# Five output buffers, an earlier split of x, and six more TensorE transposes in a windowed attention and two feed-forward layers

## The chip, the cores and the metric

The kernel runs on one core of a Trainium2 chip. The metric is the device time of one execution in microseconds (us). Three timed runs of the kernel before lie between 959.54 and 962.82 us, with a median of 962.39.

## The reference, cut to what matters

All data are fp32 (the weights of the two layers arrive as fp64). Attention looks back over 64 positions; its output, 2304 tokens of 512 values, goes through a feed-forward layer with 2048 inner columns and then through a gated one with 1536.

```python
scores = q @ k.T / sqrt(64); masked to 0 <= i - j < 64      # 4 batches, 8 heads, 576 positions
x = softmax(scores) @ v                                     # -> 2304 x 512
h = x @ w_in; x = (h * sigmoid(1.702 * h)) @ w_out          # layer A
xn = x / sqrt(mean(x * x) + 1e-6) * rms_g                   # layer B
out = (silu(xn @ w_gate) * (xn @ w_val)) @ w_out2
```

## The kernel before, in words

Every fp32 operand of a large product is kept as a high and a low part, and each product is three matmuls (high by high, high by low, low by high).

**Who sets the order.** All work is entered as operations with a cost per engine, a priority and the buffers they use. `Planner.emit` plays the program through with these costs and writes each engine's instructions in the order in which they start there. On the chip each engine then goes through its own list in that order and stops at the first instruction that must wait. SP's list holds the loads and stores; POOL's list holds, beside arithmetic, the loads of weights that are used a second time (`again`).

**Layer A** runs over six token blocks `j` (512, 256 and four of 384 tokens), with 16 steps each. Attention for the groups of 64 tokens of block `j` is laid among the matmuls of block `j - 1`. Groups are numbered 0 to 35: block 2 is groups 12 to 17, block 3 is 18 to 23. For one group TensorE computes the scores (L426), VectorE masks and reduces them (L451, L456), ScalarE takes the exponential (L461), POOL divides (L470), the probabilities are turned, and TensorE multiplies by v (L485). For groups below `NPE` = 18 the turning is four TensorE transposes into a PSUM bank (L475) and one copy out of it. From group 18 on it is a VectorE transpose in 32 by 32 squares (L518) and some ten small copies on ScalarE and POOL that put the squares in place (L310 and L312 with the tile `pts`). Along with this, the fp64 weights of layer B come in as `raw`, are narrowed on ScalarE and VectorE (L338, L342, L346, L352) and stored to DRAM as `wp` (gate and value weights, one for each unit) and `wr` (output weights). At the end of each block `a_finish` stores x and, by L704, L695 and L698, one word per token that holds its norm (`ms`, `ss`, `rs`).

**Layer B** runs over three blocks of 768 tokens, with 12 units each; even units are gates, odd ones values. The gate and value products use a scheme with seven products in place of eight (p = 0 to 6, L877 to L879, tile `bank`, two PSUM banks). Each unit thus needs seven combinations of x, prepared in `words` (`b_prep`) and split by `b_splits` into high and low parts (L310 and L808, 768 columns). The first copy after product 0 is `th<-bank` on ScalarE (L310); it frees the bank that product 2 needs. After two units, `b_down` adds their share to six accumulators of 128 tokens (L978 to L980; four tiles `y` in PSUM, two `abank`). After a block's last unit `b_finish` copies each accumulator, halved, to an SBUF tile of kind `y` (L995 on ScalarE or L997 on VectorE; there are two such tiles) and stores it (L1000).

In the first block of layer B the weights of unit n come from DRAM as fp32 (`fw<-wp`, 1 MB, L847; two buffers `fw`), are split into their frames (L310, L819; `slab` for even n, `late` for odd n), and the split form is stored as `wc` (L833) for the later blocks, which read it back by POOL's list (L837).

Of the kernel before, what the change touches and what calls it, by code (L numbers as in the profile page):

```python
# [9 lines left out]
F32 = mybir.dt.float32  # L10
# [13 lines left out]
class Buf:  # L24
    __slots__ = ("kind", "tile", "left", "users")

    def __init__(self, kind):
        self.kind, self.tile, self.left, self.users = kind, None, 0, 0
# [178 lines left out]
def window_attention_two_moe_kernel(ctx: ExitStack, tc: tile.TileContext, ins, out):  # L207
# [20 lines left out]
    NPE = gbase[3]  # L228
# [37 lines left out]
        "xa": (None, 2, [P, NK, P], F32),  # L266
        "y": (ring, 2, [P, 512], F32),
# [26 lines left out]
    def make(b):  # L294
# [8 lines left out]
        b.tile = p.tile(shape, dt, tag=b.kind, name=b.kind, bufs=n)  # L303
# [442 lines left out]
    def b_prep(j, t, prio, after):  # L746
        bufs = []
        for half in range(2):
# [3 lines left out]
            xb, rb = Buf("xa"), Buf("sq")  # L752
# [4 lines left out]
            def load_r(e, rb=rb, ja=ja, src=src):  # L757
                nc.sync.dma_start(out=make(rb)[:, 0, 0:P], in_=rs_d[ja][:, src].to_broadcast([P, P]))
# [3 lines left out]
            pl.op({"D": 0.45}, load_r, prio - 1, r=[("rs", ja)], new=[rb], after=after)  # L762
# [36 lines left out]
    def b_splits(prio):  # L799
        for p in range(7):  # L800
            hf, lf = XF + 2 * p, XF + 2 * p + 1
            st = [("st", p, t) for t in range(HT // P)]

            def hi_(e, p=p, hf=hf):
                copy("A", flat(hf), words(STAGE + p)[:, 0:2 * HT])

            def lo_(e, p=p, hf=hf, lf=lf):
                eng[e].tensor_tensor(out=flat(lf), in0=words(STAGE + p)[:, 0:2 * HT], in1=flat(hf).bitcast(F32),  # L808
                                     op=ALU.subtract)

            pl.op({"A": act(2 * HT)}, hi_, prio + p / 7, r=st, w=ftok(hf))
            pl.op(both(2 * HT), lo_, prio + p / 7, r=st + ftok(hf), w=ftok(lf), port="GV")
# [23 lines left out]
    def again(d, f, n, tok, key, prio):  # L836
        pl.op({"G": 1.2}, lambda e: nc.gpsimd.dma_start(out=frame(f)[:, :, 0:n], in_=d), prio, r=[key], w=tok,  # L837
              late=3.0)

    def b_weights(n, prio, after=()):  # L840
# [6 lines left out]
        pl.op({"D": dma(P * 8192)}, lambda e: nc.sync.dma_start(out=make(fb), in_=w32p_d[n]), prio - 0.4, new=[fb],  # L847
# [7 lines left out]

    def b_out_weights(q, prio, after=()):
        for i in range(2):
            c, f = (2 * q + i) % NB, WO + i
            if 2 * q >= NB:
# [4 lines left out]
                  prio + i - 0.4, new=[fb], r=[("w32d", "o", c), "at closed"], after=after)  # L864
# [239 lines left out]
    def ex_open(e):  # L1104
        actx.close()
        p = ctx.enter_context(tc.tile_pool(name="ex", bufs=1, side="right", reuse_waits="tile"))
        for kind in ("sb", "fw"):
            KINDS[kind] = (p, *KINDS[kind][1:])
# [124 lines left out]
```

## Time and profile before

| | |
|---|---|
| median of the timed runs | 962.39 us |
| profiled execution, its own time | 956.81 us |
| span of the trace in that execution | 955.0 us |
| busy: TensorE, VectorE, ScalarE, POOL | 912.2, 652.7, 432.7, 275.1 us |
| DMA, mean over the span | 204 GB/s |

The trace begins 1.8 us short of the execution's own time. TensorE (PE in the rows) is the engine that is nearly always busy; its idle time and the stretches with a lower granted clock (PEclk, 1.00 is 2.4 GHz and 0.50 is 1.2 GHz) are what a change can win. Layer A ends and layer B begins at about 500 us; layer B's second block begins near 660 us and its third near 810 us.

### The profile page before, as it was taken

The page shows a single profiled execution, that of the slowest core. Times are in us where ns is not written, and L with a number is a line of the kernel's source. Part 1 is how long each engine was busy: PE and PEld are TensorE (multiplying, and loading weights), DVE is VectorE, ACT ScalarE, POOL GpSimd, SP SyncE. Part 2 cuts the span into 40 slices and gives each one's busy share as a digit, 9 for nine tenths or more (in the row PEclk, how much of TensorE's full clock was granted, in tenths as well). Part 3 has the DMA queues.
Part 4 walks back from the last instruction along what each step waited for, and adds up shares of the span by engine and source line. Part 5 has one row for each costly group of instructions (what it writes and reads, how often), then busy time and mean ns, then how long its engine had stood idle before and what let it go on. Part 6 is the DMA issues. An engine that isn't in the chain of part 4 may idle for free.

```text
span 955.0 us, 15401 instructions
## 1 busy us (share of the span) xinstructions
PE 912.2 (96%) x5436; PEld 843.4 (88%) x5436; DVE 652.7 (68%) x1240; ACT 432.7 (45%) x1075; POOL 275.1 (29%) x389
## 2 busy tenths in 40 slices
PE   8999999997999999999999989998999999899997
PEld 7777789997999999899999978887999998799996
DVE  5999974474877688674477878775676567565553
ACT  6667564465566566555346333453222233222222
POOL 4111021133444345331013433372222233122210
PEclk9999999999999999999999999999899999999999
DMA  8756533357565676761759898788777676776752
GB/s 284 241 172 208 168 109 67 108 136 221 199 221 164 220 255 213 192 215 53 125 180 312 223 358 304 302 300 261 213 226 235 200 199 181 225 212 207 204 145 95
DMA packets 86536, 194.63 MB, mean 204 GB/s; under 512 B 12726, under 2 KB 36027, under 8 KB 84924
## 3 DMA queue, kind: packets, MB, share of 16 engines
q1 hardware_dynamic: 66108, 137.02, 44.5%
q0 software_dynamic: 20352, 56.63, 20.3%
q8 instruction: 43, 0.70, 0.3%
q14 instruction: 33, 0.27, 0.1%
HBM read 140.13 MB, written 53.50 MB: 203 GB/s over the span
## 4 chain that ended last, share of the span: by engine, by line
PE 41%; DMA 6%; DVE 3%; issue 1%; ACT 1%; POOL 1%; SPq 0%; ACTq 0%; POOLq 0%; DVEq 0%
PE bank L877 7%; PE bank L879 7%; PE bank L878 7%; DMA out_dram<-y 3%; PE y L978 3%; PE y L980 3%; PE y L979 3%; PE y L626 1%; DMA wc<-late 1%; PE y L627 1%; PE y L628 1%; PE bank L552 1%; PE bank L554 1%; PE bank L553 1%; PE abank L978 1%
## 5 line engine op out<-in xcount | busy, mean ns | idle before, releaser
L552 PE MATMUL bank<-xh,slab 128*128 128x384 f32 (+2 forms) x288 | 99.2, 345 | 0.5 <-DVE th L609 0.5
L554 PE MATMUL bank<-xh,slab 128*128 128x384 f32 (+2 forms) x288 | 97.2, 338 | 1.9 <-DVE slab L379 1.9
L553 PE MATMUL bank<-xl,slab 128*128 128x384 f32 (+2 forms) x288 | 97.6, 339 | 0.5 <-DVE xl L492 0.5
L626 PE MATMUL y<-gh,slab 128*128 128x384 f32 (+2 forms) x288 | 98.0, 340 | 0.0
L628 PE MATMUL y<-gh,slab 128*128 128x384 f32 (+2 forms) x288 | 96.8, 336 | 0.5 <-DVE slab L379 0.5
L627 PE MATMUL y<-gl,slab 128*128 128x384 f32 (+2 forms) x288 | 96.6, 335 | 0.0
L310 ACT ACTIVATE xh<-sb 128x384 fp32r<-128x384 f32 x72 | 36.1, 522 | 113.9 <-DVE sb L930 113.9
L878 PE MATMUL bank<-slab,late 128*128 128x384 f32 x252 | 86.8, 345 | 0.0
L902 DVE TENSOR_TENSOR gh<-gl,bank 128x384 f32<-128x384 f32 x108 | 59.3, 550 | 37.4 <-PE bank L879 37.0
L878 PE MATMUL bank<-slab,slab 128*128 128x384 f32 x252 | 84.5, 335 | 0.0
L915 ACT ACTIVATE sb<-gh 128x384 f32<-128x384 f32 x72 | 37.6, 524 | 103.3 <-DVE gh L902 103.2
L609 DVE SCALAR_TENSOR_TENSOR th<-th,bank 128x384 f32<-128x384 f32 (+2 forms) x96 | 52.6, 547 | 43.6 <-ACT th L605 43.3
L605 ACT ACTIVATE th<-bank 128x384 f32<-128x384 f32 (+2 forms) x96 | 46.4, 484 | 60.3 <-PE bank L554 53.1
L470 POOL TENSOR_TENSOR e<-e,rc 128x512 f32<-128x512 f32 x34 | 37.0, 1088 | 122.4 <-DVE rc L467 106.3
L877 PE MATMUL bank<-slab,late 128*128 128x384 f32 x180 | 63.2, 351 | 8.6 <-ACT th L310 7.8
L877 PE MATMUL bank<-slab,slab 128*128 128x384 f32 x180 | 61.6, 342 | 6.9 <-DVE gl L902 5.3
L310 ACT ACTIVATE gh<-th 128x384 fp32r<-128x384 f32 (+2 forms) x96 | 50.2, 524 | 39.0 <-DVE th L609 35.5
L879 PE MATMUL bank<-slab,late 128*128 128x384 f32 x180 | 62.5, 347 | 0.0
L338 ACT ACTIVATE raw<-raw 128x512 f32<-128x512 f32 x68 | 46.1, 680 | 33.1 <-DMA raw<-in_w_gate_dram 10.7
L879 PE MATMUL bank<-slab,slab 128*128 128x384 f32 x180 | 60.6, 337 | 0.0
L902 DVE TENSOR_TENSOR gl<-gl,bank 128x384 f32<-128x384 f32 x72 | 39.8, 552 | 28.2 <-PE bank L879 25.4
L554 PEld LDWEIGHTS bank<-xh,slab 128*128 128x128 f32 x288 | 54.3, 189 | 4.7 <-DVE slab L379 2.7
(169 smaller groups left out, 2567.3 us busy)
## 6 DMA issues: line engine op xcount, KB each, us to landing
slab<-wc POOLq DMA_DIRECT2D x36, 512.0 KB, 4.6
late<-wc POOLq DMA_DIRECT2D x36, 512.0 KB, 4.2
wp<-raw SPq DMA_DIRECT2D x24, 512.0 KB, 5.4
fw<-wp SPq DMA_DIRECT2D x12, 1024.0 KB, 7.6
late<-wo POOLq DMA_DIRECT2D x24, 512.0 KB, 5.3
q<-in_q_dram SPq DMA_DIRECT2D x36, 256.0 KB, 4.5
wc<-slab SPq DMA_DIRECT2D x18, 512.0 KB, 5.2
wc<-late SPq DMA_DIRECT2D x18, 512.0 KB, 4.3
```

The source lines that it names most:

```text
L310: nc.scalar.activation(out=out, in_=in_, func=AF.Copy)
L552: nc.tensor.matmul(h, w[:, 0, kk], xh_ring[:, kk, cols], start=(kk == 0), stop=False)
L553: nc.tensor.matmul(h, w[:, 0, kk], xl_ring[:, kk, cols], start=False, stop=False)
L554: nc.tensor.matmul(h, w[:, 1, kk], xh_ring[:, kk, cols], start=False, stop=(kk == NK - 1))
L609: nc.vector.scalar_tensor_tensor(out=th, in0=th, scalar=1.0, in1=hb.tile[:, 0:n], op0=ALU.add, op1=ALU.mult)
L626: nc.tensor.matmul(y, s[:, 0, cols], hb.tile[:, 0:n], start=first, stop=False)
L627: nc.tensor.matmul(y, s[:, 0, cols], lb.tile[:, 0:n], start=False, stop=False)
L628: nc.tensor.matmul(y, s[:, 1, cols], hb.tile[:, 0:n], start=False, stop=last)
L877: nc.tensor.matmul(h, w[:, 0, kk], xh[:, kk], start=kk == 0, stop=False)
L878: nc.tensor.matmul(h, w[:, 0, kk], xl[:, kk], start=False, stop=False)
L879: nc.tensor.matmul(h, w[:, 1, kk], xh[:, kk], start=False, stop=kk == 1)
L902: nc.vector.tensor_tensor(out=(make(to) if kind else s.tile)[:, 0:HT].bitcast(F32), in0=s.tile[:, 0:HT].bitcast(F32), in1=b.tile[:, 0:HT], ...
```

## The change

Six things are edited.

1. `NPE` goes from group 18 to group 24, so the probabilities of token block 3 are turned on TensorE.
2. Results go through five SBUF tiles in turn (one `o`, two `y`, two `sq`) and are copied by ScalarE alone.
3. The norms that layer B loads have tiles of their own (`rs`), where they used `sq` before.
4. Combinations 0 and 1 of x for the second and third block of layer B are split one unit earlier. For the second block they go into the two `fw` buffers, which are free by then; the third block finds its own frames free.
5. The last two output weights go, by POOL's list, into an `fw` buffer.
6. The planner is told other costs and priorities: `fw<-wp` ranks a unit earlier, `y<-wr` 0.8 units earlier, and a POOL load costs 0.6 in place of 1.2.

```diff
-    NPE = gbase[3]
+    NPE = gbase[4]
...
+        "rs": (None, 2, [P, 1, P], F32),
+        "o": (None, 1, [P, 512], F32),
         "y": (ring, 2, [P, 512], F32),
...
-            xb, rb = Buf("xa"), Buf("sq")
+            xb, rb = Buf("xa"), Buf("rs")
...
-            pl.op({"D": 0.45}, load_r, prio - 1, r=[("rs", ja)], new=[rb], after=after)
+            pl.op({"D": 0.45}, load_r, prio - 1, r=[("rs", ja), "at closed"], new=[rb], after=after)
...
+    xbuf = {}
+
+    def xplace(j, p, lane):
+        if (j, p) in xbuf:
+            f = xbuf[j, p].tile.rearrange("p h c l -> p (h c l)")
+            return f[:, lane * 2 * HT:(lane + 1) * 2 * HT]
+        return flat(XF + 2 * p + lane)
+
+    def xtok(j, p, lane):
+        if (j, p) in xbuf:
+            return [xbuf[j, p], (xbuf[j, p], "low")][lane:lane + 1]
+        return ftok(XF + 2 * p + lane)
+
+    def b_split(j, p, prio):
+        st = [("st", p, t) for t in range(HT // P)]
+        if j == 1 and p < 2:
+            xbuf[j, p] = Buf("fw", F32R)
+        new = [xbuf[j, p]] if (j, p) in xbuf else []
+
+        def hi_(e):
+            if new:
+                make(new[0])
+            copy("A", xplace(j, p, 0), words(STAGE + p)[:, 0:2 * HT])
+
+        def lo_(e):
+            eng[e].tensor_tensor(out=xplace(j, p, 1), in0=words(STAGE + p)[:, 0:2 * HT],
+                                 in1=xplace(j, p, 0).bitcast(F32), op=ALU.subtract)
+
+        pl.op({"A": act(2 * HT)}, hi_, prio, r=st, w=() if new else xtok(j, p, 0), new=new)
+        pl.op(both(2 * HT), lo_, prio, r=st + xtok(j, p, 0), w=xtok(j, p, 1), hold=new, port="GV")
...
-        pl.op({"G": 1.2}, lambda e: nc.gpsimd.dma_start(out=frame(f)[:, :, 0:n], in_=d), prio, r=[key], w=tok,
+        pl.op({"G": 0.6}, lambda e: nc.gpsimd.dma_start(out=frame(f)[:, :, 0:n], in_=d), prio, r=[key], w=tok,
...
-        pl.op({"D": dma(P * 8192)}, lambda e: nc.sync.dma_start(out=make(fb), in_=w32p_d[n]), prio - 0.4, new=[fb],
+        pl.op({"D": dma(P * 8192)}, lambda e: nc.sync.dma_start(out=make(fb), in_=w32p_d[n]), prio - 1.4, new=[fb], late=3.0,
...
+        if q == NBB * NU // 2 - 1:
+            wb = wobuf[q] = Buf("fw", F32R)
+            pl.op({"G": 0.01}, lambda e: make(wb), prio - 2, new=[wb])
+            for f in range(2):
+                c = (2 * q + f) % NB
+                pl.op({"G": 0.6}, lambda e, f=f, c=c: nc.gpsimd.dma_start(out=wplace(q, f), in_=wo_d[c]), prio - 2,
+                      r=[("wo", c), wb], w=[(wb, f)], late=3.0)
+            return
...
-                  prio + i - 0.4, new=[fb], r=[("w32d", "o", c), "at closed"], after=after)
+                  prio + i - 1.2, new=[fb], r=[("w32d", "o", c), "at closed"], after=after, late=2.0)
...
+    outs = []
+
     def b_finish(j, t, a, prio):
-        ob = Buf("y")
+        ob = Buf(("o", "y", "sq", "y", "sq")[len(outs) % 5])
+        outs.append(ob)
         r0 = j * BT + t * P
+        def flat_out():
+            return ob.tile.rearrange("p a c -> p (a c)") if ob.kind == "sq" else ob.tile
+
         def out_(e):
-            if e == "A":
-                nc.scalar.activation(out=make(ob), in_=a.tile, func=AF.Copy, scale=0.5)
-            else:
-                nc.vector.tensor_scalar(out=make(ob), in0=a.tile, scalar1=0.5, scalar2=None, op0=ALU.mult)
-
-        pl.op({"A": act(512, False), "V": dve(512)}, out_, prio, r=[a], new=[ob])
-        pl.op({"D": dma(P * 2048)}, lambda e: nc.sync.dma_start(out=out[r0:r0 + P], in_=ob.tile), prio, r=[ob])
+            make(ob)
+            nc.scalar.activation(out=flat_out(), in_=a.tile, func=AF.Copy, scale=0.5)
+
+        pl.op({"A": act(512, False)}, out_, prio, r=[a], new=[ob])
+        pl.op({"D": dma(P * 2048)}, lambda e: nc.sync.dma_start(out=out[r0:r0 + P], in_=flat_out()), prio, r=[ob])
...
+        if j + 1 < NBB and u == NU - 2:
+            for p in range(2):
+                b_split(j + 1, p, SA + n + 0.6 + p / 7)
         if j + 1 < NBB and u == NU - 1:
-            b_splits(SA + n + 0.7)
+            for p in range(2, 7):
+                b_split(j + 1, p, SA + n + 0.7 + p / 7)
```

The order of ScalarE's list at the end of layer B's first block, before. `y<-y` and `y<-abank` are the copies of results (L995), `th<-bank` is the copy that frees a bank after product 0, `sb<-gh` and `xh<-sb` belong to the unit's own arithmetic.

```order
L310 ACTIVATE th<-bank 128x384
L310 ACTIVATE xh<-sb 128x384 x2
L995 ACTIVATE y<-y_6062 128x512
L915 ACTIVATE sb<-gh 128x384 x2
L995 ACTIVATE y<-abank 128x512
L995 ACTIVATE y<-y_6134 128x512
L915 ACTIVATE sb<-gh 128x384 x2
L995 ACTIVATE y<-y_6154 128x512
L310 ACTIVATE th<-bank 128x384
```

The same place in the changed kernel; L1036 are the copies of results.

```order
L312 ACTIVATE th<-bank 128x384
L1036 ACTIVATE o<-y_6008 128x512
L1036 ACTIVATE y<-abank 128x512
L1036 ACTIVATE sq<-abank 128x512
L312 ACTIVATE xh<-sb 128x384
L1036 ACTIVATE y<-y_6087 128x512
L312 ACTIVATE xh<-sb 128x384
L1036 ACTIVATE sq<-y_6106 128x512
L312 ACTIVATE xh<-sb 128x384
L1036 ACTIVATE o<-y_6126 128x512
L312 ACTIVATE th<-bank 128x384
```

All six copies now stand in ScalarE's list (four did before), still ahead of the next `th<-bank`, and only the sixth takes a tile that an earlier one of the six has used.

SP's list in layer B's first block, before, from a store of unit 3's split weights to the load of unit 5's weights (`wp5`); `wc4` are the stores of unit 4's split weights.

```order
L833 DMA wc3_3_170<-late3_1306 128x1024
L698 DMA rs5_130<-ss_6128 128x3x1
L863 DMA y_6196<-wr3_146 128x512
L833 DMA wc4_0_171<-slab5_87 128x1024
L833 DMA wo2_205<-late5_1308 128x1024
L833 DMA wc4_1_172<-slab10_92 256x1x256
L833 DMA wc4_2_173<-slab7_89 128x1024
L833 DMA wc4_3_174<-slab12_94 128x1024
L847 DMA fw_6275<-wp5_136 128x2048
```

The same place in the changed kernel.

```order
L700 DMA rs5_130<-ss_6068 128x3x1
L851 DMA wc3_3_170<-late3_1306 128x1024
L865 DMA fw_6160<-wp5_136 128x2048
L851 DMA wo2_205<-late5_1308 128x1024
L898 DMA y_6206<-wr4_147 128x512
L851 DMA wc4_0_171<-slab5_87 128x1024
L851 DMA wc4_1_172<-slab10_92 256x1x256
L851 DMA wc4_2_173<-slab7_89 128x1024
L851 DMA wc4_3_174<-slab12_94 128x1024
```

The load of unit 5's weights moves ahead of the four stores of unit 4's.

VectorE's list ahead of group 20's mask, before: from the end of group 19's arithmetic (`rc`) to L451. L342 is the first VectorE step on a fresh `raw` weight.

```order
L467 RECIPROCAL rc_2611<-rc_2611 128x4
L609 SCALAR_TENSOR_TENSOR th_2609<-th_2609,bank_2564 128x384
L567 TENSOR_TENSOR gl_2632<-th_2609,gh_2630 128x384
L518 STREAM_TRANSPOSE t1_2634<-e_2579 128x512
L609 SCALAR_TENSOR_TENSOR th_2650<-th_2650,bank_2617 128x384
L567 TENSOR_TENSOR gl_2684<-th_2650,gh_2682 128x384
L342 TENSOR_SCALAR raw_2636<-raw_2636 128x512
L346 SCALAR_TENSOR_TENSOR raw_2636<-raw_2636 128x512
L609 SCALAR_TENSOR_TENSOR th_2697<-th_2697,bank_2665 128x384
L352 SCALAR_TENSOR_TENSOR raw_2636<-raw_2636 128x512
L492 TENSOR_TENSOR xl_75<-abank_2688,xh_74 128x4x64
L451 SCALAR_TENSOR_TENSOR e_2728<-abank_2703,m_rest_77 128x512
```

The same place in the changed kernel, where L344 is that first step and L453 the mask.

```order
L469 RECIPROCAL rc_2596<-rc_2596 128x4
L354 SCALAR_TENSOR_TENSOR raw_2455<-raw_2455 128x512
L611 SCALAR_TENSOR_TENSOR th_2599<-th_2599,bank_2558 128x384
L569 TENSOR_TENSOR gl_2620<-th_2599,gh_2605 128x384
L611 SCALAR_TENSOR_TENSOR th_2629<-th_2629,bank_2607 128x384
L569 TENSOR_TENSOR gl_2649<-th_2629,gh_2647 128x384
L344 TENSOR_SCALAR raw_2622<-raw_2622 128x512
L348 SCALAR_TENSOR_TENSOR raw_2622<-raw_2622 128x512
L494 TENSOR_TENSOR xl_75<-abank_2651,xh_74 128x4x64
L453 SCALAR_TENSOR_TENSOR e_2687<-abank_2664,m_rest_77 128x512
```

The VectorE transpose is gone, and the steps on the fresh weight still stand ahead of the mask. In TensorE's list 60 matmuls of 384 columns stand between group 20's scores and its product with v before; in the changed kernel there are 48, the four transposes, and 12 more.

## Rows read from the trace of the kernel before

**Rows 1.** TensorE's waits, whole span: us in total, times, longest us.

```profile
PE bank L877 <- ACT th L310: 8.8, 3, 4.2
...
PE bank L877 <- DVE gl L902: 5.3, 5, 3.1
```

**Rows 2.** Busy us by engine in stretches, granted clock, DMA share, GB/s.

```profile
150.00:200.00 50.00, 47.73 (x436) 45.85 (x436) 22.65 (x54) 24.45 (x84) 8.82 (x9) 1.00 0.38 109
235.60:241.40 5.80, 5.02 (x30) 4.74 (x31) 4.51 (x7) 3.47 (x8) 2.11 (x4) 0.51 0.85 282
500.00:650.00 150.00, 144.66 (x749) 132.20 (x748) 116.08 (x197) 68.96 (x131) 63.09 (x57) 1.00 0.88 301
668.50:674.70 6.20, 6.16 (x19) 6.17 (x20) 1.95 (x5) 0.00 (x0) 0.53 (x1) 0.50 0.80 247
677.00:795.00 118.00, 117.58 (x611) 109.06 (x612) 79.19 (x162) 31.45 (x59) 31.70 (x53) 1.00 0.75 214
814.70:818.10 3.40, 3.40 (x13) 3.40 (x12) 0.74 (x2) 0.00 (x0) 0.56 (x1) 0.50 0.30 84
948.40:955.00 6.60, 0.01 (x1) 0.00 (x0) 0.00 (x0) 1.75 (x3) 0.00 (x0) 0.71 0.41 159
```

**Rows 3.** Chain that ended last, 650 to 670 us: start, us, what.

```profile
656.28 4.37 DMA out_dram<-y
...
661.38 6.02 DMA out_dram<-y
...
667.50 0.60 ACT y L995
...
668.54 0.69 PE bank L877
```

**Rows 4.** ScalarE's timeline, 804 to 828 us: start, us, operation, [idle before, releaser].

```profile
812.67 0.60 ACT L995 ACTIVATE y<-abank 128x512 f32<-128x512 f32 x1 [4.12 <-DMA out_dram<-y]
...
825.35 0.60 ACT L995 ACTIVATE y<-y 128x512 f32<-128x512 f32 x1 [2.70 <-DMA out_dram<-y]
```

**Rows 5.** Chain that ended last, 940 to 955 us.

```profile
948.98 2.00 DMA out_dram<-y
...
951.08 0.60 ACT y L995
```

**Rows 6.** Chain that ended last, 540 to 558 us.

```profile
544.45 9.99 DMA fw<-wp
...
554.54 0.67 ACT late L310
...
557.05 0.44 PE bank L877
```

**Rows 7.** SP's timeline, 195 to 245 us.

```profile
209.29 0.39 SPq L698 DMA_DIRECT2D rs<-ss  x1
...
210.28 0.86 SPq L1136 DMA_DIRECT2D wp<-raw  x2
221.59 0.33 SPq L334 DMA_DIRECT2D raw<-in_w_val_dram  x1
```

**Rows 8.** All engines' timeline, 222 to 242 us.

```profile
225.19 0.43 DVE L342 TENSOR_SCALAR raw<-raw 128x512 int32<-128x512 int32 x1 [6.04 <-DMA raw<-in_w_val_dram]
...
232.00 1.08 POOL L470 TENSOR_TENSOR e<-e,rc 128x512 f32<-128x512 f32 x1 [2.43 <-DVE rc L467]
...
235.68 0.45 PE L485 MATMUL abank<-pts,v 128*64 128x64 f32 x2 [4.10 <-POOL pts L312]
```

**Rows 9.** TensorE's waits from 185 to 280 us.

```profile
PE abank L485 <- POOL pts L312: 4.8, 2, 4.1
```

**Rows 10.** TensorE's timeline, 142 to 168 us.

```profile
143.21 0.60 PE L475 MATMUL abank<-ident,e 128*128 128x128 f32 x4
143.56 0.36 PE L626 MATMUL y<-gh,slab 128*128 128x256 f32 x1
...
163.79 0.66 PE L475 MATMUL abank<-ident,e 128*128 128x128 f32 x4 [0.71 <-POOL e L470]
```

More of the change, by code (lines that the diff above doesn't have):

```diff
@@ L24, with __init__ @@
 class Buf:
-    __slots__ = ("kind", "tile", "left", "users")
-    def __init__(self, kind):
-        self.kind, self.tile, self.left, self.users = kind, None, 0, 0
+    __slots__ = ("kind", "tile", "left", "users", "dt")
+    def __init__(self, kind, dt=None):
+        self.kind, self.tile, self.left, self.users, self.dt = kind, None, 0, 0, dt
 class Op:
@@ L302, in make @@
         p, n, shape, dt = KINDS[b.kind]
-        b.tile = p.tile(shape, dt, tag=b.kind, name=b.kind, bufs=n)
+        b.tile = p.tile(shape, b.dt or dt, tag=b.kind, name=b.kind, bufs=n)
         return b.tile
@@ L854, in b_weights, with wplace, wtok @@
             keep(wc_d[n][f], base + f, WIDTH[f], ftok(base + f), ("wc", n, f), prio + 0.3)
-    def b_out_weights(q, prio, after=()):
+    wobuf = {}
+    def wplace(q, f):
+        return wobuf[q].tile[:, f].rearrange("p c l -> p (c l)").rearrange("p (s c) -> p s c", s=2) if q in wobuf else \
+            frame(WO + f)
+    def wtok(q, f):
+        return [wobuf[q], (wobuf[q], f)] if q in wobuf else ftok(WO + f)
+    def b_out_weights(q, prio, after=()):
+        if q == NBB * NU // 2 - 1:
[6 more added lines that the diff above has]
+            return
         for i in range(2):
@@ L874, in fn @@
             w = frame(wf)[:, :, o:o + 256].rearrange("p s (k f) -> p s k f", k=2)
-            xh, xl = block(hf), block(lf)
+            xh, xl = (xplace(j, p, lane).rearrange("p (k c) -> p k c", k=2) for lane in range(2))
             for kk in range(2):
@@ L879, in fn @@
                 nc.tensor.matmul(h, w[:, 1, kk], xh[:, kk], start=False, stop=kk == 1)
-        return pl.op({"T": 6 * mmcost(HT)}, fn, prio, r=ftok(wf) + ftok(hf) + ftok(lf), new=[hb])
+        return pl.op({"T": 6 * mmcost(HT)}, fn, prio, r=ftok(wf) + xtok(j, p, 0) + xtok(j, p, 1), new=[hb],
+                     hold=[xbuf[j, p]] if (j, p) in xbuf else ())
     halfsets = {}
@@ L970, in b_down, with fn @@
             hi, lo = uset(q, f, h)
-            wf = WO + f
             key = ("u", q % 2, f, h)
-            def fn(e, f=f, t=t, tt=tt, hi=hi, lo=lo, wf=wf):
-                s = frame(wf)
+            def fn(e, f=f, t=t, tt=tt, hi=hi, lo=lo):
+                s = wplace(q, f)
                 sl = slice(tt * P, (tt + 1) * P)
@@ L1106, in ex_open @@
         p = ctx.enter_context(tc.tile_pool(name="ex", bufs=1, side="right", reuse_waits="tile"))
-        for kind in ("sb", "fw"):
+        for kind in ("sb", "fw", "rs", "o"):
             KINDS[kind] = (p, *KINDS[kind][1:])
@@ L1166, in window_attention_two_moe_kernel @@
         a_down(s)
-    b_splits(SA - 3)
+    for p in range(7):
+        b_split(0, p, SA - 3 + p / 7)
     b_weights(1, SA - 0.5, [ups[SA - 6]])
```

17 lines of the change are left out of this document (3 added, 14 removed).

## Prediction

> **What bounds the kernel now.** I read TensorE's waits first, since that engine is nearly always busy. Two entries bear on layer B [rows 1]: three waits of together 8.8 us that end when ScalarE's `th<-bank` copy has freed a bank, the longest 4.2, and five of together 5.3 us that end with a VectorE sum, the longest 3.1. Next come the stretches with their granted clock [rows 2]. Between 677 and 795 us, inside the second block, TensorE is busy 117.58 of 118 us: away from the changes of block nothing is to be won. From 500 to 650 us, the first block, it is busy 144.66 of 150 us while the DMA engines are 88% busy at 301 GB/s. In three short stretches the clock stands at half (1.2 of 2.4 GHz): 235.6 to 241.4, 668.5 to 674.7 and 814.7 to 818.1 us. Each follows a wait, and while it lasts TensorE does half its work, so they cost about 2.8, 3.1 and 1.7 us beside the waits. The last row is the tail: 6.6 us after the last matmul.
>
> Then the chain shows what the waits hang on. At the end of the first block [rows 3] a store of a result lands after 4.37 us, the next copy takes the tile it has freed, that copy's store takes 6.02 us, and only when a third copy has had its tile (667.50) does `th<-bank` follow on the same engine and TensorE go on at 668.54. At the end of the second block ScalarE twice stands before a result copy until a store has landed, 4.12 and 2.70 us [rows 4]. So a wait for an SBUF tile becomes a wait for a PSUM bank, because ScalarE works in order.
>
> **The change part by part; the sum is made against the profiled execution, 956.8 us.**
>
> *Five tiles for results.* Only a block's sixth copy takes a tile used by one of the same block, and that copy comes a whole unit's results after the first, behind a store of some 4 to 6 us [rows 3]. So the three `th` waits go, 8.8 us [rows 1], and with them the two slow stretches after them, 3.1 + 1.7 us [rows 2]. That is 13.6 us. It is not more, since what stands between is matmuls. If the sixth copy still waits at both places I would keep half of it, 6.8. That ScalarE now copies all eighteen costs nothing: a copy is 0.60 us [rows 3], eighteen are 11 us in the whole span, and ScalarE is busy only 31.45 of 118 us in a steady stage [rows 2].
>
> *The tail.* Now the last copy (951.08) waits for a store of 2.00 us, ends at 951.7, its own store at 953.7, and the span at 955.0 [rows 5, 2]. With a free tile the last copy starts with the last matmul's end, 948.4: 0.6 + 2.0 + the same 1.3 make 3.9 us in place of 6.6. Gain 2.7; nothing excludes 1 less if the six copies queue.
>
> *Weights a unit earlier.* In the first block, unit 5's load is issued at 544.45 and lands 9.99 us later, the split follows at 554.54, and TensorE goes on at 557.05 [rows 6]. That is the 3.1 us wait. In the changed order this load stands before unit 4's four stores, so it can go about when they begin rather than after them; a few microseconds are enough. I take the 3.1 and leave the other four waits of that entry (2.2 us together). The DMA engines carry the same bytes, so no gain beyond 5.3 is open here; the loss is a rival below.
>
> *Six groups' transposes on TensorE.* Four transposes start at 143.21, and the next matmul at 143.56 [rows 10]; this matmul is also some 0.09 us slower to give way, so a group costs 0.44 us, six cost 2.6 us. What they replace lay on VectorE, ScalarE and POOL, which wait for others more than they are waited for; its removal is worth only what TensorE waited for the small copies: 4.8 us in this stage [rows 9], and the slow stretch after it, 2.8 us [rows 2]. Here I do not follow the label. Both waits are group 20's, and the row of VectorE shows where it began: idle for 6.04 us until a `raw` weight landed, at 225.19, ahead of this group's mask in its list; the division thus started only at 232.00 [rows 8]. The weight's load was issued at 221.59, when `wp` stores issued at 210.28 had given its buffer back, and these followed the one-word-per-token store `rs` of 209.29 [rows 7]. All of that order is kept, and the fresh weight is still ahead of the mask. So TensorE will now stop at the transposes instead of at `pts`. The division ends at 233.1, the transposes take 0.35 us and the copy is covered by 12 matmuls, so TensorE is free at 233.5. Before, the product with v could begin at 235.68 [rows 8], waited 0.7 again (4.8 in two waits, the first 4.1 [rows 9]) and was free at about 236.8: 3.3 us later. But the 12 matmuls that now follow the transposes were done before the wait until now, 2.3 us at 118 us for 611 matmuls in the steady stretch, 0.19 each [rows 2]. Net gain 1.0 us, with the slow clock kept. The other five groups get less room (36 or 48 matmuls between scores and transposes where 54 to 74 stood before v). Block 2's groups have that form already, and one of them waited 0.71 us for the division [rows 10]. I take 1.0 us for all five. Together +2.6 - 1.0 + 1.0 = +2.6. Bounds: if the weight lands in time, 2.6 - 4.8 - 2.8 = -5.0; if each of the five waits the 0.71, 2.6 - 1.0 + 3.6 = +5.2.
>
> On transposes the Trainium skill ("TensorE: Matmul & The Clock Gate", Part 4: PE-mode transpose) says that they do not count as work for the clock. From 150 to 200 us, with block 2's transposes among the matmuls, the granted clock is 1.00 [rows 2], so this trace does not agree; what the rule would cost is priced among the rivals.
>
> *The rest.* Two combinations split a unit ahead, the norms' own tiles, the last output weights in an `fw` buffer: the same number of instructions, at another place. The cover is a steady unit's matmuls, with 0.4 us of waits in 118 [rows 2]; I count 0. Without cover each would be a wait of the kind of the 1 to 3 us ones above.
>
> Sum: -13.6 - 2.7 - 3.1 + 2.6 = -16.8, so 940.0 for a profiled execution. The median of the runs, 962.4, stands 5.6 above the profiled one; I carry that over: **945.6 us**, 1.8% less.
>
> **The rivals.**
>
> *Group 20's wait goes as well.* If the small store lands sooner by chance of timing, the transposes are worth 5.0 where I booked a loss of 2.6: 938. For it: nothing but timing; against it: the kept order.
>
> *Stores still hold ScalarE.* If they are slower, or issued late because SP's list has loads before them, the sixth copy or the second waits, and half of the 13.6 stays: 952. Stores of 4.37 and 6.02 us beside weight loads speak for it, five tiles against it.
>
> *DMA becomes the bound of the first block (slower than before).* 88% busy leaves little. A load of 1 MB pulled ahead puts the stores of split weights back by 1 MB at 301 GB/s, 3.3 us; two units later the same frame is split again and must wait for its store. If units 4 to 11 each paid it, 8 x 3.3 = 26 us against 17 won: 972. It decides from about the sixth unit that pays. Against it: two units are 23 us (a unit has 42 matmuls of products and 18 of accumulation, 0.19 us each), far more than 3.3.
>
> *The clock.* If six groups' transposes each brought a half-clock stretch like that at 235.6 us, 2.8 us each, 17 us would be lost, in place of the one such stretch kept in the sum: 960. The Trainium skill's rule above would do this; the stretch from 150 us speaks against it.
>
> *Nothing much happens.* A new wait of ScalarE or POOL at the block changes takes most of it back: within 0.5%.
>
> **How the numbers follow.** The forecast (941 to 950) has 0.50, group 20 gone too 0.17, stores still waiting 0.12, a gain of some 6 to 9 us from several small losses 0.09, nothing much 0.06, the clock 0.02, DMA bound 0.04. 0.5%, 4.8 us, is about what a measurement of this kernel can tell from no change. Faster: 0.50 + 0.17 + 0.12 + 0.09 = 0.88. Same: 0.06 + 0.02 = 0.08. Slower: 0.04. The range reaches from a little under the second case to a little over the third, 934 to 956.
>
> **What would show it.** In the changed trace: no wait of TensorE that ends with `th<-bank` near 660 and 810 us, the clock at 1.00 there, and no result copy of ScalarE that waits for `out_dram`; a tail of about 4 us; no wait of 3 us near 554 us; a wait for the division of 3 to 5 us at group 20 before L477's transposes, with a half-clock stretch behind it; TensorE's matmuls longer by 24 transposes. I am wrong if result copies still end with a store, if layer A grows by more than 6 us, or if the first block of layer B shows waits for `wc` stores.

## The result, and the profile after

The changed kernel took 945.4 us (median of four, 944.01 to 945.68) beside 960.96 for the kernel before: ratio 0.9845, interval 0.9801 to 0.9888. Measured again in a later comparison (e5 below) it took 950.26 us, ratio 0.9886, 0.9864 to 0.9909. So it is faster by 1.1 to 1.6%, and the forecast of 945.6 was met by the first measurement; the second lies just above the 941 to 950 that I gave the forecast. Its parts were not met, as the rest shows: layer B gained more than I gave it, layer A lost more.

TensorE's waits over the whole span (total, times, longest) answer to [rows 1]:

```profile
PE abank L477 <- POOL e L472: 5.8, 2, 4.9
...
PE bank L912 <- ACT th L312: 1.9, 2, 1.7
PE bank L912 <- DVE gh L938: 1.8, 2, 0.9
...
PE bank L912 <- DVE gl L938: 0.4, 1, 0.4
```

The waits for `th<-bank` went from 8.8 us to 1.9, those for a sum to `gl` from 5.3 to 0.4. In their place the first row is group 20's wait for the division, 4.9 us, where it was forecast. I had forecast no `th` wait near 660 us; one of 1.7 us is left there (655.4 to 657.1). The stretches answer to [rows 2] (busy us by engine, granted clock, DMA share, GB/s):

```profile
150.00:189.00 39.00, 39.00 (x375) 38.19 (x375) 17.00 (x40) 18.98 (x68) 6.73 (x7) 1.00 0.34 94
193.40:196.80 3.40, 3.40 (x15) 3.40 (x15) 1.80 (x3) 0.54 (x3) 0.00 (x0) 0.50 0.63 157
234.40:237.80 3.40, 3.18 (x12) 3.18 (x13) 2.76 (x5) 1.01 (x2) 0.17 (x1) 0.50 0.78 286
377.70:381.20 3.50, 3.50 (x15) 3.50 (x16) 2.28 (x5) 0.52 (x1) 0.40 (x1) 0.51 0.84 278
408.50:411.90 3.40, 3.40 (x14) 3.40 (x15) 3.37 (x7) 1.44 (x4) 2.33 (x3) 0.50 0.36 95
500.00:650.00 150.00, 147.48 (x772) 136.28 (x771) 120.67 (x209) 72.93 (x139) 57.52 (x54) 1.00 0.87 295
650.00:670.00 20.00, 18.15 (x93) 16.18 (x92) 15.21 (x22) 6.48 (x12) 7.98 (x10) 1.00 0.73 215
677.00:795.00 118.00, 118.00 (x615) 109.86 (x614) 77.47 (x154) 32.00 (x60) 35.05 (x57) 1.00 0.78 234
805.00:825.00 20.00, 20.00 (x105) 18.55 (x105) 11.40 (x23) 7.47 (x14) 4.04 (x8) 1.00 0.93 288
939.30:943.80 4.50, 0.04 (x1) 0.00 (x0) 0.00 (x0) 0.60 (x1) 0.00 (x0) 1.00 0.50 188
```

At both block changes (650 to 670 and 805 to 825 us) the clock is now 1.00 and at the second nothing waits. The tail is 4.5 us in place of 6.6. But layer A, which had one stretch at half clock after its first 30 us, has four. Where layer A ends is read from the second `ones` matmul of each block, the last step of TensorE on a block's norms. Layer B's first products already stand before the last of these; in every run of the table below 2072 to 2074 matmuls follow it, so the mark has the same place in all of them. Before, and after (number, then duration in ns, first and last start):

```profile
L684 PE MATMUL abank<-gl,ones x6: 279/334/394, 143.0 to 525.0; 128*128 128x384 f32 x4, 128*128 128x512 f32 x1, 128*128 128x256 f32 x1
```

```profile
L686 PE MATMUL abank<-gl,ones x6: 282/336/443, 144.3 to 535.0; 128*128 128x384 f32 x4, 128*128 128x512 f32 x1, 128*128 128x256 f32 x1
```

With the durations of these last ones layer A ended 10.1 us later, layer B (from there to the last matmul) took 404.0 in place of 423.1 us, and the tail 2.1 less: together, up to rounding, the 11.2 us between the two spans. The experiments' traces, read in the same way (us; the last column is the ratio of the timed executions to the kernel before of the same comparison):

| run | end of layer A | layer B | tail | ratio, 95% |
|---|---|---|---|---|
| before | 525.3 | 423.1 | 6.6 | 1 |
| changed | 535.4 | 404.0 | 4.5 | 0.9845 (0.9801 to 0.9888) |
| e2 transposes alone | 536.1 | 425.8 | 6.6 | 1.0064 (1.0040 to 1.0089) |
| e3 five tiles alone | 523.7 | 413.0 | 4.0 | 0.9904 (0.9877 to 0.9932) |
| e4 loads earlier alone | 531.4 | 418.1 | 6.6 | 0.9924 (0.9899 to 0.9950) |
| e5 changed again | 538.3 | 406.1 | 4.4 | 0.9886 (0.9864 to 0.9909) |
| e6 changed, no transposes | 533.3 | 406.4 | 4.0 | 0.9815 (0.9795 to 0.9834) |
| e7 changed, rs from POOL | 530.4 | 404.3 | 4.0 | 0.9794 (0.9776 to 0.9812) |
| e8 both of these | 532.8 | 404.0 | 4.0 | 0.9771 (0.9747 to 0.9795) |
| e11 e6, no early splits | 530.0 | 419.8 | 4.0 | 0.9936 (0.9911 to 0.9960) |
| e12 e6, rs in rows and later | 512.5 | 403.9 | 4.0 | 0.9586 (0.9561 to 0.9611) |

Two things are to be seen. Layer B repeats to within 3 us between kernels that share its code (404.0, 406.1, 406.4, 404.3, 404.0, 403.9; before and e2, 423.1 and 425.8), so its column can be read from one trace with that uncertainty. Layer A does not: up to the end of its fifth block the kernel before and e4 have the same instructions in the same order on every engine, yet that block ended at 447.9 us in the one trace and at 454.1 in the other. What an edit does to layer A is taken from the ratios alone.

### The profile page after: what moved, and what is told of

Read it like the earlier page. It is cut to its first block, busy times and chain, and to the rows that moved or that the text cites. A ratio compares the mean times of both kernels' runs of the same rounds, so it can differ in the third digit from the quotient of the medians.

```text
span 943.8 us, 15339 instructions
## 1 busy us (share of the span) xinstructions
PE 912.6 (97%) x5460; PEld 845.6 (90%) x5460; DVE 647.1 (69%) x1241; ACT 426.9 (45%) x1039; POOL 253.3 (27%) x350
## 4 chain that ended last, share of the span: by engine, by line
PE 63%; DVE 15%; DMA 12%; ACT 5%; issue 2%; POOL 1%; SPq 0%; ACTq 0%; DVEq 0%; POOLq 0%
PE bank L912 8%; PE bank L913 8%; PE bank L914 8%; DMA wp<-raw 4%; PE bank L556 3%; PE bank L554 3%; PE bank L555 3%; PE y L1013 3%; PE y L1015 3%; PE y L1014 3%; PE y L628 3%; PE y L630 3%; PE y L629 3%; DVE raw L348 2%; PE abank L428 2%
## 5 line engine op out<-in xcount | busy, mean ns | idle before, releaser
L628 PE MATMUL y<-gh,slab 128*128 128x384 f32 (+2 forms) x288 | 99.6, 346 | 0.8 <-DVE y L653 0.8
L630 PE MATMUL y<-gh,slab 128*128 128x384 f32 (+2 forms) x288 | 97.2, 338 | 0.7 <-DVE slab L381 0.7
L913 PE MATMUL bank<-slab,late 128*128 128x384 f32 x228 | 77.1, 338 | 0.0
L913 PE MATMUL bank<-slab,slab 128*128 128x384 f32 x228 | 76.5, 336 | 0.0
L340 ACT ACTIVATE raw<-raw 128x512 f32<-128x512 f32 x68 | 46.3, 683 | 35.6 <-DMA raw<-in_w_gate_dram 10.9
L463 ACT ACTIVATE e<-e,nm 128x128 f32<-128x128 f32 x112 | 43.6, 392 | 38.6 <-DVE nm L458 37.0
L569 DVE TENSOR_TENSOR gl<-th,gh 128x384 fp32r<-128x384 f32 (+2 forms) x77 | 44.8, 581 | 22.4 <-ACT gh L312 21.9
L556 PEld LDWEIGHTS bank<-xh,slab 128*128 128x128 f32 x288 | 55.0, 191 | 5.4 <-DVE slab L381 3.3
L555 PEld LDWEIGHTS bank<-xl,slab 128*128 128x128 f32 x288 | 55.2, 192 | 2.6 <-DVE xl L494 0.6
L554 PEld LDWEIGHTS bank<-xh,slab 128*128 128x128 f32 x288 | 55.4, 192 | 2.1 <-ACT slab L312 0.2
```

Source lines behind the costliest of these rows:

```text
L554: nc.tensor.matmul(h, w[:, 0, kk], xh_ring[:, kk, cols], start=(kk == 0), stop=False)
L555: nc.tensor.matmul(h, w[:, 0, kk], xl_ring[:, kk, cols], start=False, stop=False)
L556: nc.tensor.matmul(h, w[:, 1, kk], xh_ring[:, kk, cols], start=False, stop=(kk == NK - 1))
L628: nc.tensor.matmul(y, s[:, 0, cols], hb.tile[:, 0:n], start=first, stop=False)
L630: nc.tensor.matmul(y, s[:, 1, cols], hb.tile[:, 0:n], start=False, stop=last)
L913: nc.tensor.matmul(h, w[:, 0, kk], xl[:, kk], start=False, stop=False)
```

## The experiments

### One part at a time

**Without the transposes (e1, and e6 for a trace).**

```diff
-    NPE = gbase[4]
+    NPE = gbase[3]
```

> The changed kernel, but the six groups of the fourth token block have their probabilities transposed on VectorE again. Three theories, against 945.4 us of the changed kernel. (a) The prediction's term: the transposes cost 2.6 us net, so 942.8, and layer A, which in the changed trace ends 8.4 to 9 us later than before, ends some 6 us later still. (b) All that layer A lost comes with the transposes: 936 to 937, no stretch at half clock near 377 and 408 us, layer A's last value product within 1 us of the kernel before. (c) The transposes are worth their 5.0 us and something else delays layer A: 948 to 951. What would settle it beside the time: the end of layer A in its trace.

Ratio 0.9788 (0.9763 to 0.9813), 941.9 us. I take no reading from this run's trace; e6 is the same kernel beside the changed one:

> The changed kernel with the six groups' probabilities transposed on VectorE again, once more, for a trace. Expected: 941 to 943, 4 to 6 us below the changed kernel beside it. If the cost of the transposes lies in their own six groups, the two traces part between 202 and 290 us and run level afterwards; if it lies in later groups (copies of probabilities on ScalarE behind a weight that has not landed, near 318 and 405 us), they part after 300 us.

It took 944.04 us, and the changed kernel beside it 950.26: 6.2 us, 0.0071 in the ratio. **The other way round, the transposes alone in the kernel before (e2):**

> The kernel before with the one edit that the fourth token block's six groups transpose on TensorE. Against some 961 us of the kernel before: (a) by the prediction's term 963.6; (b) if the transposes are what made layer A 8.4 to 9 us longer, 969 to 970, all of it before 525 us; (c) if the wait of group 20 goes with the small copies, 956. Group 20 should wait for the division before its transposes in (a) and (b).

968.64 against 962.86 us, so 5.8 us, near theory (b) and not (a). Three comparisons (5.5 from e1's ratio against the changed kernel's own, then 6.2 and 5.8) agree: the transposes cost about 6 us, not 2.6. The size stood just above my upper bound of 5.2. It lies in layer A: e2's layer B and tail are those of before within what a trace repeats (2.7 us and none). The two traces do not part in one place: between 203 and 456 us TensorE's waits sum to 12.5 us in e5, with the transposes, and to 10.9 in e6.

**Five result tiles alone (e3).** The kernel before with the lines of `b_finish`, the kinds `o` and `rs`, the condition `at closed` on the norm loads, and nothing else (one line of it):

```diff
-        ob = Buf("y")
+        ob = Buf(("o", "y", "sq", "y", "sq")[len(outs) % 5])
```

> The kernel before with five result tiles alone (own tiles for the norms, copies on ScalarE). By the prediction: minus 13.6 at the two block changes and minus 2.7 in the tail, 944.7 against 961, with no wait of TensorE that ends with a copy to th near 660 and 810 us and the clock at 1.00 there. By the rival that stores still hold ScalarE, half of it: 951 to 953. By a second rival, that the block changes need the earlier combinations as well (the next block's operands are then what is late), 948 to 951, with waits for split operands in the place of those for a bank.

951.13 against 962.86 us. By the ratio that is 9.2 us of 962 (6.5 to 11.8), where the five tiles and the tail together were forecast at 16.3. No result copy waits for a store and the tail is the forecast 4.0, but in the trace layer B gained 10.1 us, not 13.6. The chain of work that ended last, at the first block change (start, us, what), says why:

```profile
658.95 0.61 ACT y L1003
659.57 0.33 SPq L1006
659.96 0.47 SPq L757
660.48 7.39 DMA rs<-rs
...
668.85 0.48 DVE gh L904
669.37 0.59 PE bank L879
```

SP issues a result's store when its copy is done, and behind it in SP's list stand the loads of the next block's x and of its norms. The norm load lands after 7.39 us, the combinations of x and their splits follow, and TensorE waits 3.5 us at 665.9. This is the second rival of the expectation: with the bank free, the next block's operands are what is late. (The median stands on the border of both rivals; that no copy waits for a store decides.)

**The loads' due times alone (e4).**

```diff
-        ... in_=w32p_d[n]), prio - 0.4, new=[fb],
+        ... in_=w32p_d[n]), prio - 1.4, new=[fb], late=3.0,
...
```

The run has, beside this line, the earlier `y<-wr` (by 0.8 units) and the lower cost of POOL's loads, as in the changed kernel.

> The kernel before with only the due times of loads changed: the fw load by 1.0 earlier, the y load by 0.8 earlier, both with a bound on how early, and POOL's reloads costed at half. By the prediction minus 3.1, 957.9 against 961, the wait near 554 us gone. If the four other waits of the same kind go too (2.2 us): 955.7. If the loads push the stores back and nothing is won: 961, with another wait of 2 us or more in the first block; if they collide, above 963.

955.31 us, 7.3 us less than before (interval 4.8 to 9.7); layer B 5.0 us less in the trace. The wait near 554 us is down from 3.1 to 1.2 us (now at 560), and the second block change is nearly free of waits. At the first block change TensorE waits 4.8 us at 654 and 4.6 us at 676. So the wait that the term was made for gave 1.9 of its 3.1 us. At the second block change TensorE's waits went from 5.7 to 0.8 us and a half-clock stretch of 3.4 us went with them, which I had not connected with this edit, and the first block change got worse by the late operands of e3. Which of the three edited costs did what is open.

**Without the two combinations split early (e11).** From e6, all seven split at the block change, into their old places:

```diff
-        if j == 1 and p < 2:
+        if j == 1 and p < 0:
             xbuf[j, p] = Buf("fw", F32R)
...
-        if j + 1 < NBB and u == NU - 2:
-            for p in range(2):
-                b_split(j + 1, p, SA + n + 0.6 + p / 7)
         if j + 1 < NBB and u == NU - 1:
-            for p in range(2, 7):
+            for p in range(7):
                 b_split(j + 1, p, SA + n + 0.7 + p / 7)
```

> The changed kernel without the transposes (944.0 beside the last runs) and without the two combinations split a unit ahead: all seven are split at the block change, into the old place. By the prediction nothing: 943 to 945. By the theory that after five tiles the next thing late at a block change is the next block's operands (in the run of five tiles alone TensorE waited 3.5 us at 666 us for a product whose chain went back to a norm load of 7.4 us): 947 to 951, with waits at the two block changes that end with a sum or with split operands, and the products there not mixed with the old block's accumulations.

955.03 us: the early splits, which I had counted at nothing, are worth 0.0121 in the ratio (some 0.003 either way), 11.6 us of 961, and 13.4 us of layer B's traces. TensorE's waits in e11 show them:

```profile
PE bank L912 <- DVE gh L938: 7.2, 2, 6.3
PE bank L912 <- DVE gl L938: 6.0, 2, 4.8
```

Both long ones are at the first block change, at 653 and 675 us, each with a half-clock stretch of 6.8 us behind it. In e6 there is one wait of 1.7 us there and the clock stays at 1.00. At the second block change e11 waits for nothing either, so what the early splits are worth lies at the first.

### Why layer A lost more

**The norms' store rs (e5, e7, e8).** In the changed trace two waits of layer A that are not of the six groups look alike. The first, near 320 us (start, us, engine, line, operation, [idle before, releaser]):

```profile
318.38 0.69 ACT L340 ACTIVATE raw<-raw 128x512 f32<-128x512 f32 x1 [3.49 <-DMA raw<-in_w_gate_dram]
...
318.95 1.92 ACT L312 ACTIVATE pts<-t 32x128 f32<-32x128 f32 x6
320.01 0.30 PE L487 MATMUL abank<-pts,v 128*64 128x64 f32 x2 [1.51 <-issue]
```

ScalarE's half of the small copies stands behind a `raw` weight that has not landed, and TensorE waits for the copies: group 20's story [rows 7, 8] in a later group. The other, at 405 us, has ScalarE idle for 3.64 us before L340. In each case `rs` was stored shortly before the `wp` stores that the `raw` load waited for. This store takes long for its 1 KB (issues: KB each, median us to landing):

```profile
rs<-ss SPq DMA_DIRECT2D x1, 1.0 KB, 10.3
```

For e7 it was moved to POOL's queue:

```diff
-            nc.sync.dma_start(out=rs_d[j]...
+            nc.gpsimd.dma_start(out=rs_d[j]...
```

> The changed kernel once more, unchanged, beside the three that follow. Expected: 945 to 948, a ratio of 0.982 to 0.986 to the kernel before. Its trace shows how far single waits of layer A (near 190, 230, 318, 375 and 405 us in the first trace) repeat from one execution to the next: if layer A's end lies within 2 us of the first trace, its 9 us over the kernel before are a property of the kernel; if it moves by 4 us or more, a good part of them is the one execution that was profiled.

> The changed kernel, with the store rs issued from POOL's queue, behind the instruction that makes its values, and no longer from SP's. In the changed trace this store of single words takes 10.3 us to land, and the wp stores behind it, and the raw load that waits for them, come that much later. Theory (a), the queue holds them: the raw loads are issued 5 to 10 us earlier, the waits at group 20 (4.9) and near 318 and 405 us (2.2 and 2.5) go with two half-clock stretches of 1.7, together some 9 to 13 us: 933 to 937. Theory (b), the single words occupy the DMA engines whatever the queue: raw loads as late as now, 944 to 947. Theory (c), POOL's own queue pays for it, weight reloads later: above 948.

> Both: the transposes on VectorE again and the store rs in POOL's queue. If the transposes cost more than the 2.6 us that I gave them because they bring more weights behind that store (theory a), the difference to the run before this one shrinks to 2 to 3 us, so 931 to 934. If their cost is their own work and waits for the division, it stays at 4 to 6 us: 928 to 932 where (a) of the run before held, 939 to 942 where it did not.

e5 950.26, e7 942.06, e8 938.79 us. The changed kernel itself came out above the 945 to 948 that I expected of it, with layer A's end 2.9 us later than in the first trace; e7 lies between the ranges of theories (a) and (b). Moving the store won 0.0092 with the transposes (8.2 us; theory (a) had 9 to 13) and 0.0044 without (5.3 us). With the store out of SP's queue the transposes cost 0.0023, or 3.3 us by the medians, near my 2.6. That fits theory (a) for their extra cost, but the two differences, 0.0071 and 0.0023, each carry some 0.003, so it is likely and not settled. The mechanism in (a) is only half right. From e7's queues, the `rs` store on POOL's still took 9.9 us to land, and the stretch behind it is as empty as in e5 (first e5, then e7; granted clock, DMA share, GB/s at the end):

```profile
215.00:218.00 3.00, 3.00 (x19) 2.96 (x19) 0.84 (x2) 0.53 (x1) 0.72 (x1) 1.00 1.87 137
218.00:221.00 3.00, 3.00 (x31) 2.75 (x31) 1.11 (x2) 1.50 (x3) 0.00 (x0) 1.00 0.71 20
221.00:224.00 3.00, 3.00 (x29) 2.93 (x25) 0.00 (x0) 0.00 (x0) 0.00 (x0) 1.00 0.73 68
```

```profile
215.00:218.00 3.00, 3.00 (x21) 2.96 (x20) 0.71 (x2) 1.51 (x3) 0.00 (x0) 1.00 0.63 18
218.00:221.00 3.00, 3.00 (x33) 2.68 (x32) 0.40 (x1) 0.38 (x1) 0.00 (x0) 1.00 0.58 34
```

By the share the DMA engines are 58 to 73% busy while they move 18 to 68 GB/s; a steady stretch of layer B moves 234 GB/s at 78%. But the share adds up the times of single packets, which overlap (1.87 in the first row), and these are not the words' times. In e5's packet records the 4-byte packets that begin between 214 and 215 us, 272 of them, took some 9 ns each; it is the 4 KB packets of the two `wp` stores behind them that took 0.16 us each at first and, from 215 us on, up to 5.3 us. So the words do not fill the engines: what moves beside or behind them is held up, whichever queue they come from. That is theory (b) in its effect, and not in its reason; by what means they hold it up no run shows.

What e7 won at group 20 goes with the order of issue: the first `wp` store goes out just ahead of the words there (210.84 and 211.37), and the `raw` load at 213.55 us, in e5 at 225.35. In e8 the words go out first, on POOL's queue, and the load is as late as in e6, which has them on SP's queue (223.95). Where e8 won its 5.3 us is open. Its POOL list and its SP list (start, us):

```profile
211.56 0.78 POOL L700 DMA_DIRECT2D rs<-ss  x1
```

```profile
212.09 1.53 SPq L1175 DMA_DIRECT2D wp<-raw  x2
223.40 0.33 SPq L336 DMA_DIRECT2D raw<-in_w_val_dram  x1
```

**Without single words, first way (e9, e10).** The power is taken on the row of means, where it lies, and stored as a row:

```diff
-            nc.gpsimd.tensor_tensor(out=cb.tile[:, 0:n // P], in0=cb.tile[:, 0:n // P],
-                                    in1=mhalf.to_broadcast([P, n // P]), op=ALU.pow)
+            nc.gpsimd.tensor_tensor(out=rb.tile[0:1, 0, 0:n], in0=rb.tile[0:1, 0, 0:n],
+                                    in1=mhalf[0:1].to_broadcast([1, n]), op=ALU.pow)
```

> The changed kernel with the norms' way through single words taken out: the power is taken on the row of means where it lies, on POOL, and stored as one row, so that neither ss is loaded nor rs stored word by word. If the single words occupy the DMA engines on whatever queue (in the run with POOL's queue the engines were 58 to 64% busy at 18 to 34 GB/s while they went), this gives more than that run: 934 to 939, with the raw load of group 20 landing some 8 us earlier and no wait there above 1 us. If it was only the order in SP's queue, it gives the same 941 to 943. If the power over 384 values holds POOL for long, POOL's divisions come late and the gain goes: 944 or more.

> The same, with the six groups' transposes on VectorE again. By the theory that the transposes' extra cost was weights behind the single words, 2 to 3 us below the run before this one: 931 to 937. If they keep costing 5 to 7 us without the words, that theory falls: 928 to 933.

1250.42 and 1254.55 us: the experiment failed, for the reason named last, and far beyond what I had thought. POOL's power over 256 to 512 values of one partition (number, duration in ns: least, median, most):

```profile
L693 POOL TENSOR_TENSOR sq<-sq,mhalf x6: 41112/61642/81961, 144.3 to 778.7; 1x384 f32<-1x384 f32 x4, 1x512 f32<-1x512 f32 x1, 1x256 f32<-1x256 f32 x1
```

That is 160 ns a value, so POOL was taken up for 370 us in all. It is a reason to spread the means over 128 partitions, at the price of single words, as the kernel does. Neither run says anything on the words or the transposes.

**Second way (e12).** POOL's power stays as it is; its result, one value for each of 128 partitions and block of tokens, is turned by one small transpose on TensorE, copied, and stored as two to four rows of 512 bytes from SP's queue. From e6:

```diff
-            nc.sync.dma_start(out=rs_d[j].rearrange("one (t p) -> p (one t)", p=P), in_=cb.tile[:, 0:n // P])
+            nc.sync.dma_start(out=rs_d[j].rearrange("one (t p) -> (one t) p", p=P), in_=rb.tile[0:n // P, 0, 0:P])
...
+            nc.tensor.transpose(make(xb)[0:n // P, 0:P], cb.tile[:, 0:n // P], ident)
...
+            nc.scalar.activation(out=rb.tile[0:n // P, 0, 0:P], in_=xb.tile[0:n // P, 0:P], func=AF.Copy)
...
-        pl.op({"D": 0.45}, back, prio, r=[cb], w=[("rs", j)])
+        pl.op({"T": 0.2}, turn, prio + (1.5 if j < 5 else 0.0), r=[cb, "ident"], new=[xb])
+        pl.op({"A": 0.2}, turn_out, prio + (1.5 if j < 5 else 0.0), r=[xb], w=[rb])
+        pl.op({"D": 0.45}, back, prio + (1.5 if j < 5 else 0.0), r=[rb], w=[("rs", j)])
```

The last lines change a second thing: in all blocks but the last the store is also entered 1.5 steps later.

> The changed kernel with the transposes on VectorE again, and the norms turned into rows by one small transpose on TensorE for each block, so that rs is stored in rows of 512 bytes from SP's queue and no longer in single words; POOL's power and the load of ss stay. In the run with rs on POOL's queue the single words still kept the DMA engines 58 to 64% busy at 18 to 34 GB/s for some 10 us. If it is the words themselves that make the wp stores and raw loads late, rs lands in 2 to 4 us, group 20 waits less than 1 us, and the time is 931 to 937, below the 938.8 of that run. If the queue was what mattered and the words elsewhere cost nothing, 938 to 941. If the six small transposes and copies make TensorE wait for POOL, 942 or more.

922.06 us (921.05 to 923.51), ratio 0.9586, interval 0.9561 to 0.9611: better than the first case of the expectation, and 4.1% below the kernel before. Nearly all of it is layer A's, which ends at 512.5 us. SP's list around group 20 (start, us):

```profile
210.06 1.23 SPq L1185 DMA_DIRECT2D wp<-raw  x2
212.49 0.25 SPq L700 DMA_DIRECT2D rs<-sq  x1
214.22 0.33 SPq L336 DMA_DIRECT2D raw<-in_w_val_dram  x1
```

The `raw` load is issued at 214.22, 4 us after the first of the two `wp` stores; before it was at 221.59, 11 us after [rows 7]. Behind it, where e5 and e7 had 18 to 68 GB/s:

```profile
218.00:221.00 3.00, 3.00 (x32) 2.69 (x31) 2.28 (x5) 2.35 (x6) 0.00 (x0) 1.00 0.34 128
221.00:224.00 3.00, 3.00 (x20) 3.00 (x19) 2.96 (x5) 1.42 (x6) 2.64 (x3) 1.00 0.63 181
```

And blocks 3 to 5, of the changed kernel and of e12:

```profile
203.00:291.00 88.00, 83.08 (x564) 80.72 (x563) 59.45 (x120) 42.38 (x117) 18.35 (x25) 0.98 0.69 203
291.00:373.00 82.00, 79.56 (x534) 76.11 (x533) 59.82 (x117) 50.44 (x148) 31.92 (x55) 1.00 0.68 197
373.00:455.00 82.00, 77.90 (x510) 75.48 (x510) 52.27 (x102) 44.96 (x128) 26.70 (x46) 0.96 0.51 162
```

```profile
203.00:291.00 88.00, 88.00 (x605) 85.46 (x604) 67.59 (x132) 56.48 (x167) 36.85 (x62) 1.00 0.65 213
291.00:373.00 82.00, 82.00 (x558) 79.59 (x557) 62.33 (x121) 52.52 (x152) 39.60 (x66) 1.00 0.63 215
373.00:455.00 82.00, 82.00 (x540) 80.33 (x540) 47.89 (x94) 43.94 (x121) 19.97 (x36) 1.00 0.44 151
```

TensorE never waits there; from 29 to 920 us the clock stays at 1.00. From the end of block 2 to the end of layer A e12's trace is 19.2 us shorter than e6's, and about 17 of these are waits and half-clock stretches that e6 has and e12 has not.

Could the later place of the store alone have done this? At group 20 it could: there the `wp` stores now go out ahead of `rs`. But in the next two blocks `rs` stands ahead of `wp` in both runs, and the `raw` load follows the first `wp` store after 7.8 and 7.4 us in e6 (311.16 to 318.97, 386.71 to 394.08), after 3.4 and 2.7 in e12 (301.54 to 304.95, 372.21 to 374.87). And the packets say it for the whole of layer A: between 140 and 540 us, packets of 2 to 4 KB that took more than 1.5 us number 92 in e6, 79 and 75 in e7 and e8 with the words on POOL's queue, and 4 in e12, none of these within 20 us behind an `rs` store, where all but 2 to 7 of the others lie. So the words are the cause of the held-up transfers; how the 22 us divide between them and the new order has no run of its own. The Trainium skill ("DMA: Bandwidth & Descriptors", Specifications) puts the smallest transfer for full rate at 512 bytes; this pair of runs is in line with it, with rows of just that size beside words of 4 bytes, and tries no size between.

## Why the prediction was right, point by point

**The total** was met by luck, by errors that cancel. From trace to trace the forecast was 955.0 to 938.2 us of span (16.8 less); it became 943.8 (11.2 less). The other 5.6 us were those that I carried over from the profiled execution of before, 956.8, to the median. They were not there to carry: the changed kernel's profiled execution, 945.56, lies at its median, and of the 49 executions of the kernel before that were timed or profiled in this study, 956.8 is the second shortest (median 962.3). That step was wrong as a rule; it hid that layer A had grown. I had named "layer A grows by more than 6 us" as a sign of error, and in the traces it grew by 10. About 6 of it are the transposes; the rest is no more than one execution of layer A differs from another.

**Five tiles** (-13.6): right that the waits behind stores go, and with them the two half-clock stretches: no result copy of the changed kernel waits for a store. The `th` wait of 1.7 us that is left has another cause: ScalarE had stood idle for 3.95 us until VectorE's `sb` was done. The step that failed is "It is not more, since what stands between is matmuls", with "The rest ... I count 0". Five tiles alone gave layer B 10.1 in the trace, not 13.6, and 9.2 in the ratio with the tail, not 16.3: at the first block change the norm load and the splits were late next. The early splits made up for this and are worth 11.6 us where the other edits are made. The edits at the block change cannot be priced one by one: five tiles alone took 10.1 us off layer B, earlier loads alone 5.0, both without early splits 3.3 (e11), all together 17 to 19. I had asked what hides the splits in a steady unit, and not who waits for them at the change of blocks.

**The tail** (-2.7): -2.1 in the changed trace, -2.6 in e3. The last copies followed the last matmuls as they came.

**Weights a unit earlier** (-3.1): mis-sized. The edited costs alone gave -7.3 (4.8 to 9.7), but near 554 us, where I had placed the gain, only 1.9; of the five waits of that entry the changed kernel keeps one of 0.4 us. With -16.7 forecast for layer B by this term and the five tiles, it gained 17 to 19.

**Transposes** (+2.6): mis-sized, 5.5 to 6.2. The work itself and group 20 went as described: 24 more transposes, the wait at L477 of 4.9 us, a half-clock stretch behind it. It failed at "The other five groups get less room ... I take 1.0": I looked at the six groups, and the edit also moved the copies of later groups relative to weight loads (318 and 405 us). That this carries all of the excess is supported by e7 and e8, and not shown.

**The clock rival** found no support: six groups of transposes brought no stretch at half clock of their own, and from 150 to 189 us, with block 2's among the matmuls, the granted clock is 1.00. That row has matmuls between the transposes, so it shows that transposes laid among matmuls cost no clock here; it does not show what transposes by themselves would do, and "this trace does not agree" said too much. The new stretches all follow waits. **DMA bound** found none either: no wait for `wc` stores in the first block, with the DMA engines 87% busy.

**The root that I named and left in place** was the largest thing in the case. I had traced group 20's wait to the store `rs` [rows 7] and said that its order is kept; I never asked why a store of 1 KB delays 512 KB stores by 10 us. With rows in place of its single words, and the store a little later, e6 became 22 us faster.

## What to carry to other kernels

A wait that is removed at a change of stages shows the next late thing at the same place; price all edits there together, and ask of each which operand would be last without it. When a chain of waits ends at a tiny transfer, look at the DMA share beside the GB/s: where the share is high and little moves, transfers are being held up, here by single words, and turning the data so that they leave in rows was worth more (22 us) than moving them to another queue (5 to 8). Before comparing two single traces stage by stage, find out from kernels with the same code how far that stage repeats: here layer B to 3 us, layer A only to 6 or more.

## What was not expected of the hardware

Stores of single 4-byte words, 256 of them, took 9.9 to 10.3 us to land, on a hardware queue and on POOL's alike, and 4 KB packets beside and behind them took up to 5.3 us where 0.16 us is usual (e5). Turning 2304 such words in six stores into rows of 512 bytes, together with the later place of the store, took 22 us off the kernel (e6 to e12, 944.0 to 922.1). POOL's power takes 160 ns a value along one partition (41, 62 and 82 us for 256, 384 and 512), where 128 partitions by 4 values took 1.05 us. And the length of a wait does not by itself decide on a stretch at half clock: in the changed trace waits of 0.84 and 0.69 us at 190 us were followed by one, the same two waits in the kernel before (0.85 and 0.69 us) were not, nor was a wait of 1.72 us at 655 us. The load of `ss`, still in single words, remains in the fastest kernel; it was not tried without.
